# Reordering the SyncE queue of a hashed-attention and MLP kernel: row-turning reads and transfers ahead of stores and large loads

## The chip, the cores and the metric

The kernel runs on one core of one Trainium2 chip. The metric is device time in microseconds (us) of one execution, taken as the median of several runs.

## What is computed

There are 4 batches of 8 heads, 768 rows and head size 64. Queries and keys are hashed into buckets by the signs of six projections. A query attends only to keys of its own bucket; the attention output, with its heads side by side, is the x of a normalised two-layer MLP with a residual.

```
mask   = q_bucket[:, :, :, None] == k_bucket[:, :, None, :]
scores = np.where(mask, scale * q @ k.T, -1e9)
x      = softmax(scores) @ v                    # to (4, 768, 512)
xn     = (x - mean(x)) / sqrt(var(x) + 1e-6) * g_ln
out    = x + relu(xn @ w_ch1) @ w_ch2           # 512 -> 2048 -> 512
```

## The kernel before

**Units.** The 768 rows of each batch are cut into three units of 256 rows, so that there are 12 units u = 0 to 11. A unit goes through attention for two groups of four heads (g = 0, 1), then normalisation, then the MLP.

**Steps.** For each batch b and head group g, k and q rows are loaded in one transfer of 768 KB each (`LX.s.b.g.t`, line 508, with t = 0 for q and 1 for k) and transposed in 32x32 blocks on VectorE (`tu`, line 304). TensorE computes the projections (`hm`, line 526), VectorE makes sign bits of them (`bt`, line 307), and SyncE writes the bits to DRAM (`mw`, line 544) and reads them back in another arrangement with four small DMAs (`mr.s.b.g.i`, line 547, i = 0 to 3), into the tile G. These are the row-turning reads. The scores (`S`, line 570) start each accumulation with four matmuls that read all four parts of G, then ScalarE takes the exponential (`E`, line 576), and the values are multiplied in (`A`, line 595).

For each unit, VectorE normalises rows into xc (`ce.v.u.t`, line 630; t = 0, 1 are the two halves of 128 rows; a small GpSimd step `rs`, lines 635 and 636, comes ahead of it). From unit 2 on a DMA transpose turns each half into xnT (`fl.s.u.t`, line 639); these are the row-turning transfers. The first MLP layer (`F.t.u.p`, line 659, eight pieces p of a unit) reads both halves of xnT; its result is taken through relu by ScalarE or VectorE (`R`, lines 667 and 669). The second layer is a seven-product scheme on sums of blocks (`P`, line 725; sums `ss`, line 710; VectorE adds the products to x with `Y`, line 730). Last, four stores write the unit (`O.s.u.c`, line 744; 128 KB each; the last unit's at line 742). Values come with `lv.s.b.h.c` (line 467, 192 KB each).

**Order.** Nothing is reordered by a scheduler. A string ORDER lists all work word by word: name, engine, arguments. The engine letters are v VectorE, a ScalarE, p GpSimd, s SyncE, t TensorE. Each engine executes its words in the order of the string, and an instruction that waits holds back all behind it on the same engine. All words with an s are DMA issues on the one queue of SyncE (SPq in the profile). Another fixed string gives the buffer of each tile: TensorE's F, P and other small accumulators share two PSUM buffers, S and A share three.

```
with tc.manual_schedule():
    for word in ORDER.split():
        name, eng, *args = word.split(".")
        OPS[name](ENGINES[eng], *map(int, args))
```

Of the kernel before, what the change touches and what calls it, by code (L numbers as in the profile page):

```python
# [46 lines left out]
S.t.19.2 F.t.1.6 E.a.18.0 rs.p.2 F.t.1.3 CA.p.1.1.1 E.a.19.0 S.t.21.2 O.s.0.0 lv.s.1.4.1  # L47
E.a.19.1 A.t.19.2 E.a.21.0 R.v.1.6 sw.v.3.0 sw.v.2.0 E.a.21.1 F.t.1.0 R.a.1.0 lv.s.2.0.3
R.v.1.3 ce.v.2.1 sw.v.4.0 lv.s.1.4.0 ce.v.2.0 F.t.1.5 A.t.20.2 S.t.22.2 fl.s.2.1 tu.v.2.0.0.2
F.t.1.4 R.a.1.5 cv.p.1.4.0 A.t.18.2 LX.s.2.0.1 E.a.22.0 R.v.1.4 F.t.1.2 sp.t.1.0 sc.v.1.0  # L50
na.v.3.0 E.a.22.1 S.t.23.2 F.t.1.7 R.a.1.2 R.v.1.7 E.a.23.1 cv.v.1.4.2 E.a.23.0 F.t.1.1
sw.v.1.0 fl.s.2.0 R.a.1.1 nb.v.3.0 S.t.24.2 E.a.24.0 E.a.24.1 on.p.2 P.t.1.2 Y.v.1.2
F.t.2.1 R.a.2.1 su.p.1.4 S.t.26.2 lv.s.2.4.0 O.s.0.1 O.s.0.3 A.t.23.2 ss.v.1.1 P.t.1.1
P.t.1.5 ss.v.1.3 ss.v.1.2 tu.v.2.0.1.2 E.a.26.1 E.a.26.0 Y.v.1.1 lv.s.2.0.1 P.t.1.6 A.t.22.2
S.t.25.2 tu.v.2.0.0.3 ss.v.1.4 lv.s.2.4.3 E.a.25.0 Y.v.1.5 tu.v.2.0.0.0 Y.v.1.6 P.t.1.3 Y.v.1.3
# [13 lines left out]
F.t.3.7 R.a.3.7 F.t.3.0 tu.v.2.1.1.0 E.a.33.0 S.t.37.2 E.a.37.1 tu.v.2.1.1.1 E.a.37.0 tu.v.2.1.0.0  # L69
tu.v.2.1.1.3 tu.v.2.1.1.2 hm.t.2.1 O.s.2.0 CA.v.2.1.0 LX.s.3.0.0 bt.v.2.1 mw.s.2.1 mr.s.2.1.1 mr.s.2.1.3  # L70
S.t.38.2 F.t.3.5 R.v.3.0 A.t.34.2 R.a.3.5 F.t.3.3 CA.v.2.1.1 R.a.3.3 tu.v.3.0.1.0 E.a.38.1
A.t.35.2 F.t.3.4 A.t.33.2 O.s.2.2 nb.v.5.0 F.t.3.1 mr.s.2.1.2 R.a.3.4 na.v.5.1 tu.v.3.0.0.3
F.t.3.2 lv.s.3.4.1 E.a.38.0 R.a.3.1 rs.p.4 ce.v.4.1 S.t.36.2 P.t.3.2 R.a.3.2 E.a.36.1
nb.v.5.1 su.p.2.4 ss.v.3.1 Y.v.3.2 P.t.3.1 E.a.36.0 mr.s.2.1.0 S.t.39.2 E.a.39.1 E.a.39.0
O.s.2.3 ce.v.4.0 Y.v.3.1 nc.v.5.0 A.t.37.2 P.t.3.5 ss.v.3.2 ss.v.3.4 fl.s.4.1 LX.s.3.1.0
A.t.36.2 Y.v.3.5 cv.v.2.4.0 P.t.3.6 Y.v.3.6 P.t.3.3 A.t.38.2 ss.v.3.3 S.t.40.2 Y.v.3.3
E.a.40.0 E.a.40.1 P.t.3.7 nc.v.5.1 Y.v.3.7 tu.v.3.0.0.1 fl.s.4.0 F.t.4.3 ag.v.5.0 R.v.4.3
P.t.3.4 Y.v.3.4 O.s.3.1 O.s.3.0 S.t.41.2 E.a.41.1 E.a.41.0 sp.t.2.0 sc.v.2.0 F.t.4.0
ag.v.5.1 rs.p.5 F.t.4.4 R.a.4.4 na.v.6.0 R.v.4.0 O.s.3.3 ce.v.5.1 fl.s.5.1 S.t.44.2
E.a.44.1 tu.v.3.0.1.3 F.t.4.5 A.t.41.2 F.t.4.6 A.t.40.2 tu.v.3.0.0.2 E.a.44.0 R.a.4.6 tu.v.3.0.1.2  # L80
# [42 lines left out]
O.s.8.3 F.t.9.6 R.a.9.6 nb.v.11.0 ss.v.9.1 ss.v.9.2 S.t.70.2 E.a.70.1 A.t.71.2 ss.v.9.3  # L123
O.s.8.2 A.t.69.2 P.t.9.2 Y.v.9.2 ss.v.9.4 P.t.9.1 fl.s.10.0 E.a.70.0 Y.v.9.1 A.t.70.2
na.v.11.1 nb.v.11.1 fl.s.10.1 F.t.10.7 P.t.9.6 R.a.10.7 Y.v.9.6 nc.v.11.0 P.t.9.5 P.t.9.7
Y.v.9.5 Y.v.9.7 nc.v.11.1 P.t.9.3 Y.v.9.3 P.t.9.4 Y.v.9.4 O.s.9.3 O.s.9.0 O.s.9.2
F.t.10.6 R.a.10.6 ag.v.11.1 F.t.10.1 O.s.9.1 ag.v.11.0 rs.p.11 ce.v.11.0 fl.s.11.0 F.t.10.0
R.a.10.1 R.a.10.0 F.t.10.5 R.a.10.5 F.t.10.4 F.t.10.3 R.a.10.4 R.a.10.3 ce.v.11.1 fl.s.11.1
F.t.10.2 R.a.10.2 P.t.10.2 Y.v.10.2 F.t.11.4 R.a.11.4 ss.v.10.1 ss.v.10.2 P.t.10.1 Y.v.10.1
ss.v.10.4 P.t.10.5 Y.v.10.5 P.t.10.6 P.t.10.3 ss.v.10.3 Y.v.10.6 P.t.10.7 Y.v.10.3 F.t.11.0  # L130
R.a.11.0 Y.v.10.7 P.t.10.4 Y.v.10.4 O.s.10.2 F.t.11.2 R.a.11.2 F.t.11.5 R.a.11.5 F.t.11.7
# [10 lines left out]
    E="012302132023132032103230103231032031230120302123031230120321013202120320",  # L142
# [10 lines left out]
    rs="012102102102",  # L153
# [635 lines left out]
```

## Time and profile before

| | us |
|---|---|
| median of 3 runs | 294.99 |
| lowest and highest of them | 294.71, 295.28 |
| profiled execution, own time | 294.86 |
| its span, first to last instruction | 293.2 |
| mean granted TensorE clock | 1.000 |

The span is what the views of the profile divide up; the profiled execution's own time is 1.66 us longer than its span. In the profile PE is TensorE's matmuls, PEld its weight loads, DVE VectorE, ACT ScalarE, POOL GpSimd, SPq SyncE's DMA issues. A timeline row gives start, duration, engine, line, operation, output and inputs, the count of merged instructions, and in brackets the idle time before it with what ended it. Matmuls are pipelined, so that one row's duration reaches over the start of the next; the distance from start to start is what a group costs.

### The profile page before, as it was taken

The numbers are of one execution on the slowest core, as the hardware profiler recorded it, in microseconds if no ns is written. First come the engines' busy times: TensorE is split into PE (matmuls) and PEld (weight loads), VectorE is DVE, ScalarE is ACT, GpSimd is POOL, SyncE is SP. The second block draws the span as 40 slices with busy tenths as digits, with TensorE's granted clock in tenths as the row PEclk, the third lists the DMA queues.
The fourth block names the chain that finished last, engine by engine and source line by source line (L and its number), as shares of the span: only waits on it lengthen the run. The fifth ranks groups of instructions, "written<-read, shape, count | busy, mean of one in ns | idle before, by whom it ended". The sixth has DMA issues, their size and how long they took to land.

```text
span 293.2 us, 10524 instructions
## 1 busy us (share of the span) xinstructions
PE 285.6 (97%) x4650; PEld 227.7 (78%) x4650; DVE 206.8 (71%) x474; ACT 206.2 (70%) x236; POOL 54.0 (18%) x88
## 2 busy tenths in 40 slices
PE   8999999999999999999999999999999999999994
PEld 4677778648788887878778778877888878897883
DVE  4757899996769795797667995866666654773433
ACT  4689999998966978784865896887793694515240
POOL 5261325222423005000300107210010010000000
PEclk9999999999999999999999999999999999999999
DMA  6999997747744692362330352230410402304022
GB/s 223 302 319 250 216 277 133 139 134 171 174 122 131 134 307 76 127 189 51 98 82 1 83 132 63 60 61 3 92 37 2 74 2 52 78 6 104 2 72 73
DMA packets 31055, 34.10 MB, mean 116 GB/s; under 512 B 15521, under 2 KB 27809, under 8 KB 31010
## 3 DMA queue, kind: packets, MB, share of 16 engines
q1 hardware_dynamic: 25938, 28.72, 35.6%
q0 software_dynamic: 4224, 4.19, 8.9%
q8 instruction: 36, 0.59, 0.9%
q10 hardware_dynamic: 848, 0.53, 0.7%
q14 instruction: 9, 0.07, 0.1%
HBM read 27.86 MB, written 6.88 MB: 118 GB/s over the span
## 4 chain that ended last, share of the span: by engine, by line
PE 91%; DMA 3%; DVE 2%; SPq 1%; ACT 1%; issue 0%; ACTq 0%; DVEq 0%
PE f L659 27%; PE sc L570 18%; PE X L725 13%; PE acc L595 12%; PE Yb L725 7%; PE hp L526 3%; PE Ya L725 3%; PE hf L394 3%; PE f L674 2%; PE warm L363 1%; ACT E L576 1%; DMA G<-Bd 1%; DMA Bd<-B 1%; PE warm L366 1%; DMA xnT<-xc 1%; SPq L547 1%
## 5 line engine op out<-in xcount | busy, mean ns | idle before, releaser
L576 ACT ACTIVATE E<-sc,bias_sb 128x1024 bf16<-128x1024 f32 x144 | 153.1, 1111 | 36.0 <-PE sc L570 32.6
L659 PE MATMUL f<-xnT,w_sb 128*128 128x256 bf16 x768 | 94.2, 273 | 0.7 <-DMA xnT<-xc 0.6
L659 PEld LDWEIGHTS <-w_sb 128*128 128x128 bf16 x768 | 71.4, 98 | 13.6 <-issue 5.7
L667 ACT ACTIVATE hb<-f 128x512 bf16<-128x512 f32 x67 | 39.6, 598 | 34.5 <-PE f L659 34.5
L570 PE MATMUL sc<-qb,kb 32*128 32x256 bf16 x1152 | 52.5, 267 | 0.0
L595 PEld LDWEIGHTS <-E 128*128 128x128 bf16 x1152 | 40.8, 98 | 4.0 <-issue 2.5
L595 PE MATMUL acc<-vaug,E 128*128 128x65 bf16 x1152 | 43.7, 194 | 0.1
L570 PE MATMUL sc<-G 6*128 6x256 bf16 (+1 forms) x576 | 42.7, 273 | 1.1 <-ACT E L576 0.8
L725 PEld LDWEIGHTS <-hb 128*128 128x128 bf16 x352 | 33.4, 98 | 5.4 <-issue 1.3
L570 PEld LDWEIGHTS <-kb 32*128 32x128 bf16 x1152 | 30.5, 93 | 1.5
L635 POOL TENSOR_SCALAR rs<-mv 128x2 f32<-128x2 f32 x12 | 3.3, 277 | 150.4 <-DVE mv L624 150.4
L730 DVE TENSOR_TENSOR x<-X,x 128x256 f32<-128x256 f32 x44 | 18.4, 419 | 16.5 <-PE X L725 16.3
L570 PEld LDWEIGHTS <-G 6*128 6x128 bf16 (+1 forms) x576 | 16.0, 91 | 16.7 <-issue 13.3
L725 PEld LDWEIGHTS <-S 128*128 128x128 bf16 x264 | 25.0, 98 | 4.8 <-issue 1.4
L669 DVE TENSOR_SCALAR hb<-f 128x512 bf16<-128x512 f32 x29 | 19.7, 681 | 12.0 <-PE f L659 11.8
L304 DVE STREAM_TRANSPOSE T<-X 128x384 f32<-128x384 f32 (+2 forms) x52 | 26.1, 535 | 0.0
L725 PE MATMUL Yb<-w_sb,S 128*128 128x256 bf16 x176 | 22.9, 273 | 0.0
L608 DVE SCALAR_TENSOR_TENSOR y<-vsB,acc 128x520 f32<-128x520 f32 x24 | 16.5, 689 | 8.1 <-PE acc L595 7.8
L725 PE MATMUL X<-wt,hb 128*128 128x256 bf16 x168 | 21.8, 273 | 0.0
L617 DVE TENSOR_TENSOR x<-y,rc 128x512 f32<-128x512 f32 x24 | 17.8, 742 | 0.8
L621 DVE BATCH_NORM_STATS2 st<-x 128x6 f32<-128x256 f32 x48 | 17.4, 412 | 0.2
L730 DVE TENSOR_TENSOR x<-Yb,x 128x256 f32<-128x256 f32 x22 | 9.2, 420 | 9.5 <-PE Yb L725 9.5
(95 smaller groups left out, 268.3 us busy)
## 6 DMA issues: line engine op xcount, KB each, us to landing
out_dram<-x SPq DMA_DIRECT2D x45, 128.0 KB
X<-in_k_dram SPq DMA_DIRECT2D x7, 768.0 KB
vn<-in_v_dram SPq DMA_DIRECT2D x24, 192.0 KB
X<-in_q_dram SPq DMA_DIRECT2D x6, 768.0 KB
w_sb<-in_moe_w_ch_dram POOLq DMA_DIRECT2D x8, 512.0 KB, 10.8
vn<-in_v_dram SPq DMA_DIRECT2D x2, 768.0 KB
X<-in_q_dram SPq DMA_DIRECT2D x2, 512.0 KB
Bd<-B SPq DMA_DIRECT2D x6, 96.0 KB
```

The lines of the kernel that those rows point to most:

```text
L304: nc.vector.transpose(d[:, j], s[:, j, kj0 : kj0 + n])
L570: nc.tensor.matmul(sc(s, i // 2)[:, i % 2, 256 * kk : 256 * kk + 256], lh, rh, start=(rep == 0), stop=(rep == 2), skip_group_check=True,)
L576: nc.scalar.activation(E(s)[:, heads(h)], sc(s, h), AF.Exp, scale=EXP_SCALE, bias=bias_sb)
L595: nc.tensor.matmul(acc[:, qt, (D + 1) * i : (D + 1) * (i + 1)], E(s)[:, i, 256 * kk + P * qt : 256 * kk + P * qt + P], vaug(u // 3)[:, 4 * ...
L608: nc.vector.scalar_tensor_tensor(yt(u, g), vs, EPS_ROW, made[f"acc{u}{g}"][:, :, :A], op0=AOP.mult, op1=AOP.add,)
L617: nc.vector.tensor_tensor(xo, a[:, :, :, 0:D], rc.to_broadcast([P, 2, 4, D]), op=AOP.mult)
L621: nc.vector.bn_stats(stats(u)[:, qt, g], xt(u)[:, qt, 256 * g : 256 * g + 256])
L659: nc.tensor.matmul(f1[:, n].rearrange("p (t x) -> p t x", t=2), w1_sb[:, dt, P * nt : P * nt + P], xnT(u)[:, :, dt], start=(dt == 0), stop ...
L667: nc.scalar.activation(hb(u)[:, 2 * p : 2 * p + 2], f1, AF.Relu)
L669: eng.tensor_scalar_max(hb(u)[:, 2 * p : 2 * p + 2], f1, 0.0)
L725: nc.tensor.matmul(f2, lh[:, n], rh[:, n], start=(first and n == 0), stop=(n == 7), skip_group_check=True)
L730: nc.vector.tensor_tensor(x, made[f"{prod(u, k)}{u}"], x, op=AOP.add)
```

## The change

In four places of ORDER words with an s stand elsewhere. No word is added or taken out, and on TensorE, VectorE, ScalarE and GpSimd the order of the instructions is the same as before.

1. `LX.s.2.0.1` (768 KB of keys) goes from between `fl.s.2.1` and `fl.s.2.0` to behind `fl.s.2.0`.
2. `mr.s.2.1.2` and `mr.s.2.1.0` go ahead of `O.s.2.2` and `lv.s.3.4.1`: the four row-turning reads of batch 2, group 1, then stand together.
3. `LX.s.3.1.0` (768 KB of queries) goes from between `fl.s.4.1` and `fl.s.4.0` to behind `fl.s.4.0`.
4. The four stores `O.s.9.*` go from ahead of `fl.s.11.0` and `fl.s.11.1` to behind both.

```
-F.t.1.4 R.a.1.5 cv.p.1.4.0 A.t.18.2 LX.s.2.0.1 E.a.22.0 R.v.1.4 F.t.1.2 sp.t.1.0 sc.v.1.0
-na.v.3.0 E.a.22.1 S.t.23.2 F.t.1.7 R.a.1.2 R.v.1.7 E.a.23.1 cv.v.1.4.2 E.a.23.0 F.t.1.1
-sw.v.1.0 fl.s.2.0 R.a.1.1 nb.v.3.0 S.t.24.2 E.a.24.0 E.a.24.1 on.p.2 P.t.1.2 Y.v.1.2
+F.t.1.4 R.a.1.5 cv.p.1.4.0 A.t.18.2 E.a.22.0 R.v.1.4 F.t.1.2 sp.t.1.0 sc.v.1.0 na.v.3.0
+E.a.22.1 S.t.23.2 F.t.1.7 R.a.1.2 R.v.1.7 E.a.23.1 cv.v.1.4.2 E.a.23.0 F.t.1.1 sw.v.1.0
+fl.s.2.0 LX.s.2.0.1 R.a.1.1 nb.v.3.0 S.t.24.2 E.a.24.0 E.a.24.1 on.p.2 P.t.1.2 Y.v.1.2
...
-A.t.35.2 F.t.3.4 A.t.33.2 O.s.2.2 nb.v.5.0 F.t.3.1 mr.s.2.1.2 R.a.3.4 na.v.5.1 tu.v.3.0.0.3
-F.t.3.2 lv.s.3.4.1 E.a.38.0 R.a.3.1 rs.p.4 ce.v.4.1 S.t.36.2 P.t.3.2 R.a.3.2 E.a.36.1
-nb.v.5.1 su.p.2.4 ss.v.3.1 Y.v.3.2 P.t.3.1 E.a.36.0 mr.s.2.1.0 S.t.39.2 E.a.39.1 E.a.39.0
-O.s.2.3 ce.v.4.0 Y.v.3.1 nc.v.5.0 A.t.37.2 P.t.3.5 ss.v.3.2 ss.v.3.4 fl.s.4.1 LX.s.3.1.0
-A.t.36.2 Y.v.3.5 cv.v.2.4.0 P.t.3.6 Y.v.3.6 P.t.3.3 A.t.38.2 ss.v.3.3 S.t.40.2 Y.v.3.3
-E.a.40.0 E.a.40.1 P.t.3.7 nc.v.5.1 Y.v.3.7 tu.v.3.0.0.1 fl.s.4.0 F.t.4.3 ag.v.5.0 R.v.4.3
+A.t.35.2 F.t.3.4 A.t.33.2 mr.s.2.1.2 mr.s.2.1.0 O.s.2.2 nb.v.5.0 F.t.3.1 R.a.3.4 na.v.5.1
+tu.v.3.0.0.3 F.t.3.2 lv.s.3.4.1 E.a.38.0 R.a.3.1 rs.p.4 ce.v.4.1 S.t.36.2 P.t.3.2 R.a.3.2
+E.a.36.1 nb.v.5.1 su.p.2.4 ss.v.3.1 Y.v.3.2 P.t.3.1 E.a.36.0 S.t.39.2 E.a.39.1 E.a.39.0
+O.s.2.3 ce.v.4.0 Y.v.3.1 nc.v.5.0 A.t.37.2 P.t.3.5 ss.v.3.2 ss.v.3.4 fl.s.4.1 A.t.36.2
+Y.v.3.5 cv.v.2.4.0 P.t.3.6 Y.v.3.6 P.t.3.3 A.t.38.2 ss.v.3.3 S.t.40.2 Y.v.3.3 E.a.40.0
+E.a.40.1 P.t.3.7 nc.v.5.1 Y.v.3.7 tu.v.3.0.0.1 fl.s.4.0 LX.s.3.1.0 F.t.4.3 ag.v.5.0 R.v.4.3
...
-Y.v.9.5 Y.v.9.7 nc.v.11.1 P.t.9.3 Y.v.9.3 P.t.9.4 Y.v.9.4 O.s.9.3 O.s.9.0 O.s.9.2
-F.t.10.6 R.a.10.6 ag.v.11.1 F.t.10.1 O.s.9.1 ag.v.11.0 rs.p.11 ce.v.11.0 fl.s.11.0 F.t.10.0
-R.a.10.1 R.a.10.0 F.t.10.5 R.a.10.5 F.t.10.4 F.t.10.3 R.a.10.4 R.a.10.3 ce.v.11.1 fl.s.11.1
+Y.v.9.5 Y.v.9.7 nc.v.11.1 P.t.9.3 Y.v.9.3 P.t.9.4 Y.v.9.4 F.t.10.6 R.a.10.6 ag.v.11.1
+F.t.10.1 ag.v.11.0 rs.p.11 ce.v.11.0 fl.s.11.0 F.t.10.0 R.a.10.1 R.a.10.0 F.t.10.5 R.a.10.5
+F.t.10.4 F.t.10.3 R.a.10.4 R.a.10.3 ce.v.11.1 fl.s.11.1 O.s.9.3 O.s.9.0 O.s.9.2 O.s.9.1
```

The compiled program also makes each DMA of the hardware queues wait for the eighth DMA before it, since eight completion counters take turns. Moving a DMA moves these waits with it.

## Prediction

> **What bounds the kernel now.** I read the page first, then the waits of TensorE, then the timelines around each of them. From the page:
>
> ```profile
> span 293.2 us, 10524 instructions
> ...
> PE 285.6 (97%) x4650; PEld 227.7 (78%) x4650; DVE 206.8 (71%) x474; ACT 206.2 (70%) x236; POOL 54.0 (18%) x88
> ...
> PE 91%; DMA 3%; DVE 2%; SPq 1%; ACT 1%; issue 0%; ACTq 0%; DVEq 0%
> ```
>
> TensorE is busy in 285.6 of 293.2 us, and 91% of the chain that ended last runs through it. The other engines have 30% or more to spare. The change touches only SyncE, so it can pay only where TensorE itself stood still for one of SyncE's DMAs. The chain has 3% for DMA, so such places exist. The waits of PE from 60 us to the end (engine and line, what it waited for, us in total, times, longest):
>
> ```profile
> PE f L659 <- DMA xnT<-xc: 0.6, 1, 0.6
> PE sc L570 <- DMA G<-Bd: 0.3, 1, 0.3
> ```
>
> These two are all that PE itself shows in this stretch: once for a transposed half of xnT, once for a row-turning read into G. PEld shows a third, below. The idle time in brackets understates a stall, since matmuls overlap: the tail of one group hides the first part of a gap. So I measure each stall by the distance between the starts of two groups, against the same pair of groups where nothing waits.
>
> **Place 1: the load of keys behind the second transpose.** SyncE's timeline, then DVE's making of the second half of xc:
>
> ```profile
> 69.86 1.20 SPq L639 DMA_TRANSPOSE xnT<-xc  x1
> 71.11 0.58 SPq L508 DMA_DIRECT2D X<-in_k_dram  x1
> 71.79 1.20 SPq L639 DMA_TRANSPOSE xnT<-xc  x1
> ```
> ```profile
> 70.31 0.54 DVE L630 TENSOR_SCALAR xc<-x,mv,rs 128x512 bf16<-128x512 f32 x1
> ```
>
> The xc that `fl.s.2.0` reads is done at 70.85, so the transpose can be issued at 71.11 in the load's place, 0.68 us earlier. What waits for it, in the timelines of PE, of PEld, and of DVE for the load's reader:
>
> ```profile
> 77.72 1.05 PE L725 MATMUL Ya<-w_sb,hb 128*128 128x256 bf16 x8
> 78.75 1.05 PE L659 MATMUL f<-xnT,w_sb 128*128 128x256 bf16 x8
> ```
> ```profile
> 78.74 0.77 PEld L659 LDWEIGHTS <-w_sb 128*128 128x128 bf16 x8 [0.26 <-DMA xnT<-xc]
> ```
> ```profile
> 81.07 0.57 DVE L304 STREAM_TRANSPOSE T<-X 128x384 f32<-128x384 f32 x1
> ```
>
> F.2.1 starts 1.03 us after the product ahead of it. Undisturbed, eight matmuls of this shape take 0.87 or 0.88 us to the next group (126.48 to 127.36, quoted below, is 0.88). I take 0.87, and the stall is **0.16 us**. The transpose landed at 78.74 at the latest, 6.95 us after its issue. With 6.95 us again it would land at 78.06, ahead of the 78.59 at which TensorE would be ready; with the 2.48 us of another transpose (below) at 73.6. So the whole 0.16 goes. Bounds: 0 to 0.26, the bracket.
>
> The load's cost is what is added. Its issue moves to about 71.11 + 1.20 + 0.05 = 72.36, which is 1.25 us later. How long it travels, by the DMA column (last two: DMA share, GB/s):
>
> ```profile
> 76.00:77.00 1.00, 1.00 (x14) 0.72 (x15) 0.82 (x2) 1.00 (x2) 0.70 (x1) 1.00 0.04 4
> ```
>
> From 76.00 almost nothing moved, so the load issued at 71.11 had its bytes across within 4.9 us, hence by 77.3 in the new order. Its first reader is the DVE transpose at 81.07, `tu.v.2.0.1.2`, which comes to 80.9 once TensorE runs 0.16 us earlier: 3.6 us of cover. Even if the load took the 6.95 us of the transpose it lands at 79.3, with 1.6 us left. One more wait moves with the load: the value load `lv.s.2.0.0` is the eighth DMA behind it now and waits for its landing; that load's buffer is not read before the other quarters of the tile have come. I cost the moved load at nothing.
>
> The Trainium skill, page "DMA: Bandwidth & Descriptors", section "Queues, rings and completion order", says that each DMA engine consumes the descriptors of a ring in order. The trace agrees in so far as the transpose behind the load took 6.95 us and another one, with no load just ahead, 2.48. By that rule the load now pays for the transpose put ahead of it; the sum stays as it is, since 1.6 us or more of cover is left, but this is what makes the slower rival below possible.
>
> **Place 2: the four reads of G together.** PE's timeline at the stall, the same pair of groups where nothing waits, and SyncE's timeline:
>
> ```profile
> 126.48 1.05 PE L725 MATMUL Ya<-w_sb,hb 128*128 128x256 bf16 x8
> 127.36 1.04 PE L725 MATMUL X<-w_sb,hb 128*128 128x256 bf16 x8
> 128.70 0.29 PE L570 MATMUL sc<-G 6*128 6x256 bf16 x4 [0.30 <-DMA G<-Bd]
> ```
> ```profile
> 112.31 1.04 PE L725 MATMUL X<-wt,hb 128*128 128x256 bf16 x8
> 113.28 0.29 PE L570 MATMUL sc<-G 6*128 6x256 bf16 x4
> ```
> ```profile
> 123.82 0.43 SPq L744 DMA_DIRECT2D out_dram<-x  x1
> 124.30 0.67 SPq L547 DMA_DIRECT2D G<-Bd  x1
> 125.08 0.37 SPq L467 DMA_DIRECT2D vn<-in_v_dram  x1
> 125.50 0.67 SPq L547 DMA_DIRECT2D G<-Bd  x1
> 126.22 0.44 SPq L744 DMA_DIRECT2D out_dram<-x  x1
> 126.70 1.27 SPq L639 DMA_TRANSPOSE xnT<-xc  x1
> 128.01 0.57 SPq L508 DMA_DIRECT2D X<-in_q_dram  x1
> ```
>
> The undisturbed distance is 113.28 - 112.31 = 0.97, here it is 1.34: a stall of **0.37 us**. The chain of waits puts it on the last of the four reads:
>
> ```profile
> 125.50 3.16 DMA G<-Bd
> ```
>
> In the new order the third read is issued at 123.82 and the fourth at 123.82 + 0.67 + 0.05 = 124.54, which is 0.96 earlier. With the same 3.16 us it lands at 127.70, and TensorE is ready at 128.33; it should be shorter, since the value load and one store are no longer between. So all 0.37 goes. Lower bound 0.30 by the bracket; above 0.37 there is nothing. The next limit is a PSUM buffer that ACT's exponential of S.36 gives back for A.37, which comes behind S.39:
>
> ```profile
> 126.60 2.12 ACT L576 ACTIVATE E<-sc,bias_sb 128x1024 bf16<-128x1024 f32 x2 [0.19 <-PE sc L570]
> ```
>
> It ends at 128.72, after S.39 starts but before its end, so it hinders nothing at 128.33. The store and the value load move back by two issues (about 1.4 and 0.7 us) and their sum with the next store fills the same time, so the transpose at 126.70 stays. The value load's readers need the other quarters of that tile too, of which the next, `lv.s.3.4.3`, is issued here:
>
> ```profile
> 165.01 0.43 SPq L467 DMA_DIRECT2D vn<-in_v_dram  x1
> ```
>
> So its 0.7 us cost nothing.
>
> **Place 3: the load of queries behind the transpose.** The load is issued at 128.01 now. The transpose takes its place, as soon as its xc is done (about 128.5), and the load follows at about 129.7, 1.7 us later. TensorE shows no wait for this transpose, so nothing is gained. The load's first reader, in DVE's timeline:
>
> ```profile
> 148.18 0.83 DVE L304 STREAM_TRANSPOSE T<-X 128x128 f32<-128x128 f32 x2
> ```
>
> At 129.7 + 6.95 = 136.7 it has landed by a long estimate from place 1: 11 us of cover. Cost **0**.
>
> **Place 4: four stores behind the last two transposes.** SyncE, the chain, DVE's making of xc (both halves), PE, and ACT's last relu of unit 10:
>
> ```profile
> 262.91 3.07 SPq L744 DMA_DIRECT2D out_dram<-x  x4
> 266.09 2.51 SPq L639 DMA_TRANSPOSE xnT<-xc  x2
> 277.67 1.73 SPq L744 DMA_DIRECT2D out_dram<-x  x4
> ```
> ```profile
> 267.39 2.48 DMA xnT<-xc
> ```
> ```profile
> 264.20 1.00 DVE L630 TENSOR_SCALAR xc<-x,mv,rs 128x512 bf16<-128x512 f32 x2 [1.13 <-POOL rs L636]
> ```
> ```profile
> 268.37 1.04 PE L725 MATMUL Ya<-w_sb,hb 128*128 128x256 bf16 x8
> 270.01 1.03 PE L659 MATMUL f<-xnT,w_sb 128*128 128x256 bf16 x8 [0.60 <-DMA xnT<-xc]
> ```
> ```profile
> 268.57 0.60 ACT L667 ACTIVATE hb<-f 128x512 bf16<-128x512 f32 x1 [0.28 <-PE f L659]
> ```
>
> F.11.4 starts 1.64 us after the product; undisturbed it is 0.87: a stall of **0.77 us**. The first xc half is done near 264.7 and the second at 265.2, while SyncE is still issuing stores until 265.98. In the new order the first transpose goes out at about 264.75, the second 1.3 us later at 266.05, where it is 267.39 now; with the same 2.48 us it lands at 268.53, ahead of 269.24. What is late next is F.11.4's PSUM buffer, which the relu at 268.57 gives back at 269.17: just in time. So 0.77 goes; bounds 0.60 by the bracket and 0.77. The stores go out from about 267.3 and need 3.1 us. No buffer is reused behind them (unit 9's x is never overwritten), the next stores come at 277.67, and the end lies at 293.2: cost 0.
>
> **Sum.** 0.16 + 0.37 + 0.77 = 1.30 us, and 0 for what is moved back. TensorE is the chain between the places, and the work of DVE, ACT and SyncE at the later places follows it, so that each gain moves all that comes after. The profiled execution took 294.86: 294.86 - 1.30 = 293.56, and its span 293.2 - 1.3 = 291.9. The median of the runs is 0.13 higher, so I forecast 294.99 - 1.30 = 293.69, rounded **293.7 us** (0.44% less). 0.2%, or 0.6 us, is about what a measurement of this kernel can tell from no change.
>
> **Rivals.**
>
> *Only the last stall pays.* The first two gains (0.53 us) lie 140 us and more ahead of the end; ACT or DVE may hold TensorE at some later wait, and then only place 4 counts: 294.99 - 0.77 = 294.2, or 294.4 with 0.60. For it: ACT is busy 70% on average, and at place 2 its exponential ends only shortly ahead of A.37. Against it: PE waits for no other engine after 60 us in the list above.
>
> *The waits come back.* F.11.4 has the PSUM buffer of the relu as its next limit and the xc halves behind GpSimd's step; if the second transpose again lands near 270 because the first one's issue is held, all that is left is places 1 and 2: 294.99 - 0.53 = 294.5, no difference that can be told. Against it: xc is ready 1.3 us before the issue now.
>
> *The load of keys becomes the bound: slower.* The transpose of place 1 took 6.95 us although little moved from 76.00 on, and the trace does not tell what held it. If that hold now falls on the load, with two transposes ahead of it in the queue, it lands late and DVE stands at 81.07, with `Y` and the sums for TensorE's products behind it. It decides from a landing at 80.9, that is 8.5 us after the issue. Each further us costs TensorE up to one: 11.8 us of travel cost 3.3, less the 1.14 of places 2 and 4, so 294.99 + 2.2 = 297.2; 10.3 us cost 1.8, giving 295.7. Against it: 6.95 us is the longest seen here.
>
> *The change does not do what it says.* The order of SyncE's issues shows the four moves and the other engines unchanged, so I give it 1 in 100, at 295.0.
>
> **How the numbers follow.** The forecast has 0.66, with its own range 293.2 to 294.1 (the bounds of the three terms, 0.90 to 1.40, and 0.4 more below for the spread of the runs). Only the last stall: 0.17, of which 0.11 lies under 294.4 and counts as faster, 0.06 within 0.2%. The waits come back: 0.07, within. No move: 0.01, within. The late load: 0.09, of which 0.08 slower and 0.01 within. Faster is 0.66 + 0.11 = 0.77; same 0.06 + 0.07 + 0.01 + 0.01 = 0.15; slower 0.08. The range reaches over the forecast and most of the second case: 293.2 to 294.5, leaving out some 2 in 10.
>
> **What would show it.** In the profile after, PE's waits for xnT and G after 60 us are gone; F.2.1 follows its product by 0.87, S.39 by 0.97, F.11.4 by 0.87; the chain has no DMA between 119 and 129 and none at 267; TensorE's last product ends 1.3 us earlier. Wrong would be: a DVE wait for X near 81 or 148, a wait of the same length at F.11.4 with another releaser, or TensorE gaining at the three places and losing the time at ACT later.

## The result, and the profile after

| | before | after |
|---|---|---|
| median of 15 runs, us | 294.99 | 293.46 |
| lowest to highest, us | 293.51 to 297.25 | 292.44 to 295.73 |
| profiled execution, own time, us | 294.86 | 293.50 |
| its span, us | 293.2 | 291.8 |

The ratio after to before is 0.9944, 95% interval 0.9921 to 0.9967: 1.65 us less, between 0.97 and 2.33 (the two medians lie 1.53 us apart). From the page after, the span, the busy times, and the chain that ended last by engine:

```profile
span 291.8 us, 10523 instructions
...
PE 285.1 (98%) x4648; PEld 228.0 (78%) x4650; DVE 205.9 (71%) x474; ACT 206.1 (71%) x236; POOL 53.8 (18%) x88
...
PE 95%; DVE 2%; ACT 1%; issue 0%; ACTq 0%; DVEq 0%
```

DMA has left the chain altogether, and PE is 95% of it where it was 91%. PE's waits over the whole span of the kernel after:

```profile
PE warm L363 <- DVE bias_sb L320: 1.1, 1, 1.1
PE sc L570 <- ACT E L576: 0.8, 3, 0.4
PE ft L644 <- DVE xc L628: 0.2, 1, 0.2
```

Neither xnT nor G is among them. PE's timeline after, around the three places (answers for three windows):

```profile
77.65 1.05 PE L725 MATMUL Ya<-w_sb,hb 128*128 128x256 bf16 x8
78.53 1.04 PE L659 MATMUL f<-xnT,w_sb 128*128 128x256 bf16 x8
...
127.14 1.04 PE L725 MATMUL X<-w_sb,hb 128*128 128x256 bf16 x8
128.11 0.29 PE L570 MATMUL sc<-G 6*128 6x256 bf16 x4
...
267.78 1.04 PE L725 MATMUL Ya<-w_sb,hb 128*128 128x256 bf16 x8
268.65 1.04 PE L659 MATMUL f<-xnT,w_sb 128*128 128x256 bf16 x8
...
286.48 1.04 PE L725 MATMUL Yc<-wt,hb 128*128 128x256 bf16 x8
```

The three distances from start to start are 0.88, 0.97 and 0.87 us, where they were 1.03, 1.34 and 1.64. Against before, F.11.4 comes 1.36 us earlier (268.65 for 270.01). The last product, which stood at 287.83 before, comes 1.35 us earlier, so nothing was given back in the 18 us between. SyncE after:

```profile
69.80 2.52 SPq L639 DMA_TRANSPOSE xnT<-xc  x2
72.37 0.57 SPq L508 DMA_DIRECT2D X<-in_k_dram  x1
...
119.50 0.34 SPq L544 DMA_DIRECT2D Bd<-B  x1
122.66 2.80 SPq L547 DMA_DIRECT2D G<-Bd  x4
...
264.22 2.50 SPq L639 DMA_TRANSPOSE xnT<-xc  x2
```

Both pairs of transposes go out back to back. The key load is at 72.37 (forecast 72.36), and the transposes of unit 11 start at 264.22 instead of 266.09. The key load's first reader on DVE, without a wait in brackets:

```profile
81.00 0.57 DVE L304 STREAM_TRANSPOSE T<-X 128x384 f32<-128x384 f32 x1
```

The traces also keep the increments of the DMAs' completion counters, which none of the views above prints. The last increment of a DMA is its landing; where a landing below stands in no line, it was read from these counters. By them the key load landed 4.48 us after its issue, at 76.85, and so 4.15 us ahead of this reader.

### The profile page after: what moved, and what is told of

The parts are those of the page before. It is cut to its first block, busy times and chain, and to the rows that moved or that the text cites. A ratio compares the mean times of both kernels' runs of the same rounds, so it can differ in the third digit from the quotient of the medians.

```text
span 291.8 us, 10523 instructions
## 1 busy us (share of the span) xinstructions
PE 285.1 (98%) x4648; PEld 228.0 (78%) x4650; DVE 205.9 (71%) x474; ACT 206.1 (71%) x236; POOL 53.8 (18%) x88
## 4 chain that ended last, share of the span: by engine, by line
PE 95%; DVE 2%; ACT 1%; issue 0%; ACTq 0%; DVEq 0%
PE f L659 30%; PE sc L570 18%; PE X L725 13%; PE acc L595 12%; PE Yb L725 7%; PE Ya L725 3%; PE hp L526 3%; PE hf L394 3%; PE f L674 2%; PE warm L363 1%; ACT E L576 1%; PE warm L366 1%; DVE xnT L652 0%; PE hf L405 0%; PE vp L487 0%; PE Yc L725 0%
## 5 line engine op out<-in xcount | busy, mean ns | idle before, releaser
L617 DVE TENSOR_TENSOR x<-y,rc 128x512 f32<-128x512 f32 x24 | 16.6, 692 | 0.8
L480 POOL TENSOR_TENSOR t<-vn 128x768 f32<-128x768 f32 x6 | 11.4, 1896 | 25.0 <-DMA vn<-in_v_dram 25.0
```

Of the source, the lines that this page charges most:

```text
L617: nc.vector.tensor_tensor(xo, a[:, :, :, 0:D], rc.to_broadcast([P, 2, 4, D]), op=AOP.mult)
```

## The experiments

A stall below is the distance from start to start less that of an undisturbed pair (0.87, 0.97 and 0.87 us), as in the prediction. In some of these kernels ORDER is wrapped in fewer lines, so that a code line has a number 7 lower. Where a kernel has one run, the table sets it beside 295.08, the median of 23 runs of the kernel before measured with it.

**Each place alone**, on the kernel before. The edit of the first:

```
-fl.s.2.1 ... LX.s.2.0.1 ... fl.s.2.0 R.a.1.1
+fl.s.2.1 ... fl.s.2.0 LX.s.2.0.1 R.a.1.1
```

> Only place 1: the key load LX.s.2.0.1 behind fl.s.2.0, all else as before. Each stall is read as the distance from start to start of two neighbouring groups of TensorE. My theory (each place removes its own stall, and the gains add): the distance from the product Ya to F.2.1 falls from 1.03 to 0.87 us, the stalls at S.39 (1.34) and F.11.4 (1.64) stay within 0.1 us, and the span is 0.1 to 0.2 us shorter than before's 293.2, with the scatter of single executions on top. The rival that early gains are given back: 0.87 at F.2.1, but a stall at S.39 or F.11.4 that is longer by as much. The rival that the key load becomes the bound: DVE shows a wait for X at 81 us.

The second, third and fourth:

```
-O.s.2.2 nb.v.5.0 F.t.3.1 mr.s.2.1.2 ... lv.s.3.4.1 ... mr.s.2.1.0
+mr.s.2.1.2 mr.s.2.1.0 O.s.2.2 nb.v.5.0 F.t.3.1 ... lv.s.3.4.1 ...
```
```
-fl.s.4.1 LX.s.3.1.0 ... fl.s.4.0
+fl.s.4.1 ... fl.s.4.0 LX.s.3.1.0
```
```
-O.s.9.3 O.s.9.0 O.s.9.2 ... O.s.9.1 ... fl.s.11.0 ... fl.s.11.1
+... fl.s.11.0 ... fl.s.11.1 O.s.9.3 O.s.9.0 O.s.9.2 O.s.9.1
```

> Only place 2: the four row-turning reads of batch 2, group 1, stand together. My theory: the distance from the product to S.39 falls from 1.34 to 0.97 us, F.2.1 keeps its 1.03 and F.11.4 its 1.64 within 0.1 us, the time falls by 0.37 us (ratio 0.9987, too small for the interval). If early gains are given back: the time stays, and F.11.4 or a later group waits 0.37 us longer.

> Only place 3: the query load LX.s.3.1.0 behind fl.s.4.0. My theory: nothing changes, all three stalls stay (1.03, 1.34, 1.64 us within 0.1) and DVE shows no wait for X near 148 us. The rival that moving a load is never free: DVE waits for X at 148 us, or the span is over 0.5 us longer.

> Only place 4: the four stores of unit 9 behind both transposes of unit 11. My theory: the distance from the product Ya to F.11.4 falls from 1.64 to 0.87 us, the stalls at F.2.1 and S.39 stay within 0.1 us, the time falls by 0.77 us (ratio 0.9974). The rival that only the last stall pays: the ratio is that of the whole change, 0.9944. The rival that the wait comes back with another releaser: F.11.4 still 1.2 us or more behind its product, ratio near 1.

| kernel | stall at F.2.1 | at S.39 | at F.11.4 | time |
|---|---|---|---|---|
| before | 0.16 | 0.37 | 0.77 | 1 |
| place 1 alone | 0.02 | 0.79 | 0.39 | one run, 295.1 us beside 295.08 |
| place 2 alone | 0.43 | 0 | 0 | 0.9977 (0.9952 to 1.0001) |
| place 3 alone | 0.02 | 1.18 | 0.66 | one run, 295.34 us beside 295.08 |
| place 4 alone | 0.01 | 0.93 | 0 | 0.9983 (0.996 to 1.0006) |
| after | 0.01 | 0 | 0 | 0.9944 (0.9921 to 0.9967) |

The edits at places 2 and 4 leave no stall at their own place, as expected. The load of place 3 was free: DVE's list of waits in that run has no wait for X near 148. But my expectation that the other stalls would stay within 0.1 us failed in every row. Place 2 alone shows nothing at F.11.4, where its order is still the old one, and S.39 stalled for 0.79 to 1.18 us in three kernels that leave it as it was. PE's timeline in the kernel with place 3 alone:

```profile
127.19 1.04 PE L718 MATMUL X<-w_sb,hb 128*128 128x256 bf16 x8
129.34 0.29 PE L563 MATMUL sc<-G 6*128 6x256 bf16 x4 [1.11 <-DMA G<-Bd]
```

and in the kernel with place 2 alone, at the stores' place that it leaves untouched:

```profile
268.74 1.04 PE L718 MATMUL Ya<-w_sb,hb 128*128 128x256 bf16 x8
269.61 0.60 PE L652 MATMUL f<-xnT,w_sb 128*128 128x256 bf16 x4
```

Both have the same code at that place as before, with 2.15 us instead of 1.34, and 0.87 instead of 1.64. Either one change moves a stall elsewhere, or a stall is drawn anew in each execution.

**The kernel before, twice more**, unchanged.

> The kernel before once more, unchanged, for a second profile. In the four runs that change one place, the stalls at the unchanged places were not those of before's profile: 0.01 to 0.43 us at F.2.1 (before 0.16), 0.79 to 1.18 at S.39 (before 0.37), 0 to 0.66 at F.11.4 (before 0.77). My theory now: each execution draws its stalls anew, from how long SyncE's stores take to issue and how long the bits take to land in DRAM; the kernel before would show 0 to 0.5, 0.3 to 1.3 and 0 to 0.8 us, not the same three numbers again. The rival: before's three numbers are fixed (within 0.1 us: 0.16, 0.37, 0.77) and the single-place kernels differ because of their change.

> A third profile of the kernel before, for the same question: drawn anew (three stalls that again differ by 0.2 us or more from the other two profiles, S.39 by 0.3 to 1.3 us) or fixed at 0.16, 0.37 and 0.77 us within 0.1.

The stalls were 0.01, 1.26 and 0.38 us in the second profile, and 0.01, 1.43 and 0.05 in the third. The rival falls: with no change of the code the numbers are not 0.16, 0.37 and 0.77 again. The two new profiles are alike at the first two places and differ by 0.33 us at the third, so I had asked for more scatter between them than there was, and 1.43 lies beyond the 1.3 that I gave for S.39. What is drawn at place 2 shows in SyncE's timeline of the first profile of before, quoted in the prediction from 123.82 on, which begins

```profile
117.00 0.36 SPq L508 DMA_DIRECT2D X<-in_q_dram  x1
119.71 0.34 SPq L544 DMA_DIRECT2D Bd<-B  x1
122.38 1.39 SPq L547 DMA_DIRECT2D G<-Bd  x2
```

and in the third:

```profile
116.07 0.36 SPq L508 DMA_DIRECT2D X<-in_q_dram  x1
118.78 0.34 SPq L544 DMA_DIRECT2D Bd<-B  x1
122.53 1.39 SPq L547 DMA_DIRECT2D G<-Bd  x2
```

From the write of the bits to the first read it took 2.67 us in one and 3.75 in the other, 1.08 more; the stall at S.39 is 1.06 longer (1.43 against 0.37). So the time until the write lands goes straight into the stall. It is not a time of the small write by itself. The first line of both views is a load of 768 KB (`LX.s.3.0.0`), issued 2.71 us ahead of the write, and in all twelve profiles of this document the write lands 0.30 to 0.33 us behind that load. The six profiles with the old order at place 2, in us:

| kernel | load LX.s.3.0.0, issue to landing | stall at S.39 |
|---|---|---|
| before | 5.03 | 0.37 |
| place 1 alone | 5.34 | 0.79 |
| place 4 alone | 5.60 | 0.93 |
| place 3 alone | 6.06 | 1.18 |
| before, second | 6.08 | 1.26 |
| before, third | 6.09 | 1.43 |

The stall rises with the time of this load in all six. No run moves the load, so it is not shown that moving it would end the stall, and what makes it take 5.03 us in one execution and 6.09 in another stays open.

At place 4 it is the issue of one DMA that is drawn. In the second and then in the third profile of before:

```profile
263.16 1.72 SPq L744 DMA_DIRECT2D out_dram<-x  x4
265.06 3.40 SPq L639 DMA_TRANSPOSE xnT<-xc  x2
```

```profile
263.04 1.72 SPq L744 DMA_DIRECT2D out_dram<-x  x4
264.95 3.06 SPq L639 DMA_TRANSPOSE xnT<-xc  x2
```

In both the four stores take 1.72 us and leave SyncE free when xc is ready, but then the first transpose takes long to issue: 2.09 and 1.76 us instead of 1.20, and F.11.4 stalls 0.38 and 0.05. In the first profile it was the fourth store (1.77 us of the 3.07), and the stall was 0.77. In each of the six profiles with the old order at place 4 one of these five issues takes 1.39 to 2.09 us. What holds it is not shown by an experiment. The traces show a coincidence: in all six, one packet of 16 KB on the instruction queue, 0.90 to 1.59 us long, starts at 264.04 to 264.90 while the stores are under way; two or three stores get the last of their 16 counts 1.0 to 1.9 us behind the others; and the held issue ends 0.2 to 1.1 us behind the packet. In the kernel after, the packet runs from 263.44 to 264.66 with no store under way, and no issue is held. No run moves the packet.

**A load ahead of both transposes of unit 11**, in the kernel after:

```
-fl.s.11.0
+LX.s.3.1.1 fl.s.11.0
```

> The changed kernel with one more 768 KB load on SyncE's queue right ahead of the two transposes of unit 11 (it reads keys of batch 3 again into a buffer that nobody reads any more). It tells whether a transfer ahead in the queue costs the transposes its issue or its bytes. If only the issue counts (0.4 to 0.6 us, and SyncE is free from 250 us on, so that even this is hidden): F.11.4 stays 0.87 us behind its product, time as the changed kernel. If the transposes stand behind the load's bytes (a load of this size needed up to 4.9 us from issue to quiet): the load, issued as soon as the transposes of unit 10 are out, at about 252 us, is over before the xc halves are ready at 263.6, so it must again be without effect. Both say no effect here unless SyncE's issue itself is held; an F.11.4 later than 1.0 us behind its product would show that.

Stalls 0.01, 0 and 0; ratio to before 0.9948 (0.9919 to 0.9977). The load was out at 251.93, 11.5 us before the transposes. The run tells nothing about order in the queue, as its expectation had to admit; it stands as a second timing of the change's three places.

**The key load later still**, in the kernel after:

```
-fl.s.2.0 LX.s.2.0.1 ... O.s.0.1 O.s.0.3
+fl.s.2.0 ... O.s.0.1 O.s.0.3 LX.s.2.0.1
```

> The changed kernel with the key load LX.s.2.0.1 moved on, behind the stores O.s.0.1 and O.s.0.3: its issue goes from 72.37 to about 78.7 us. It prices the rival in which this load becomes the bound. By the 4.9 us from issue to quiet that a load of this size needed, it lands near 84 us, while its reader on DVE stands at 81.0. My theory: DVE waits 2 to 4 us for X, and TensorE loses nearly that, less some 0.5 us of room at the products behind it: 1.5 to 3.5 us longer than the changed kernel, that is near or above before (ratio 0.999 to 1.006). If the cover was longer than I read it: no wait of DVE, time as the changed kernel (0.9944).

The ratio to before is 1.0103 (1.0058 to 1.0147), beyond my upper end of 1.006, which the interval just reaches. From the answers of SyncE, DVE and PE:

```profile
79.38 0.45 SPq L501 DMA_DIRECT2D X<-in_k_dram  x1
```
```profile
85.89 0.58 DVE L297 STREAM_TRANSPOSE T<-X 128x384 f32<-128x384 f32 x1 [4.18 <-DMA X<-in_k_dram]
```
```profile
82.22 1.04 PE L718 MATMUL Yb<-w_sb,S 128*128 128x256 bf16 x8
86.83 1.87 PE L718 MATMUL X<-wt,S 128*128 128x256 bf16 x8 [3.57 <-DVE x L723]
88.49 1.09 PE L588 MATMUL acc<-vaug,E 128*128 128x65 bf16 x16
```

The mechanism of the slower rival is real. The load landed 6.41 us after its issue, and DVE stood 4.18 us for it. The 4.9 us that I had read from the DMA column were too short: by the completion counters the same load had needed 6.39 us in the first profile of before. TensorE lost 86.83 - 82.22 - 0.87 = 3.74 us, which is DVE's wait less 0.4 us of room. But it lost more behind that: the eight matmuls at 86.83 took 1.66 us to the next group instead of 0.87. The windows say why (the number before the last two is the granted clock):

```profile
84.00:86.00 2.00, 0.00 (x0) 0.00 (x0) 0.11 (x1) 0.00 (x0) 0.00 (x0) 1.00 1.04 261
86.00:87.00 1.00, 0.17 (x2) 0.11 (x2) 1.00 (x3) 0.00 (x0) 0.00 (x0) 0.75 0.82 222
87.00:88.00 1.00, 1.00 (x6) 0.76 (x5) 1.00 (x3) 0.00 (x0) 0.00 (x0) 0.50 0.32 118
88.00:89.00 1.00, 1.00 (x13) 0.82 (x12) 0.91 (x3) 0.00 (x0) 0.45 (x1) 0.50 0.00 0
89.00:90.00 1.00, 1.00 (x23) 0.79 (x24) 0.16 (x1) 0.00 (x0) 1.00 (x1) 0.54 0.00 0
```

After 3.57 us of idleness the granted clock was 0.50 for about 3.4 us, from about 86.5 on. That does not happen in every execution: of the nine runs behind the ratio, three have a mean granted clock of 1.000 and took 295.65 to 295.91 us, which is inside what I expected (1.5 to 3.5 us above the changed kernel's 293.46); the six with 0.991 to 0.994 took 296.79 to 299.81.

**A load between two transposes, and a load ahead of the last read**, both in the kernel after:

```
-fl.s.11.1
+LX.s.3.1.1 fl.s.11.1
```

> The changed kernel with one more load of 768 KB between the two transposes of unit 11 (keys of batch 3 again, into a buffer that nobody reads any more), as place 1 had a load between its two. Issue alone: the second transpose goes out 0.65 us later, near 266, and lands 2.5 us after: F.11.4, ready at 268.6, stalls 0 to 0.2 us. Bytes ahead in the queue: the load is quiet up to 4.9 us after its issue at about 265.2, so the transpose lands at 270.5 to 272.7 and F.11.4 stalls 2 to 4 us, with more lost behind if the granted clock falls as it did after the stall of 3.7 us in the late-keys run.

```
-mr.s.2.1.2 mr.s.2.1.0 ... fl.s.4.0 LX.s.3.1.0
+mr.s.2.1.2 LX.s.3.1.0 mr.s.2.1.0 ... fl.s.4.0
```

> The changed kernel with the query load LX.s.3.1.0 (768 KB) moved ahead of the last of the four row-turning reads of place 2. Issue alone: that read goes out 0.6 us later, near 125.4, and lands at most 3.2 us after: S.39, ready at 128.1, stalls 0 to 0.5 us. Bytes ahead in the queue: the read lands behind the load, 129.5 to 131.5, and S.39 stalls 1.5 to 3.5 us, that is 2.5 to 4.5 us from start to start of the two groups.

PE and the chain with the load between the transposes:

```profile
267.22 1.04 PE L718 MATMUL Ya<-w_sb,hb 128*128 128x256 bf16 x8
270.51 1.03 PE L652 MATMUL f<-xnT,w_sb 128*128 128x256 bf16 x8 [2.26 <-DMA xnT<-xc]
```
```profile
265.57 4.81 DMA xnT<-xc
```

and with the load ahead of the read:

```profile
127.91 1.04 PE L718 MATMUL X<-w_sb,hb 128*128 128x256 bf16 x8
131.85 0.29 PE L563 MATMUL sc<-G 6*128 6x256 bf16 x4 [2.90 <-DMA G<-Bd]
```
```profile
126.74 5.07 DMA G<-Bd
```

The stalls are 3.29 - 0.87 = 2.42 us and 3.94 - 0.97 = 2.97 us, inside what the bytes would give (2 to 4, 1.5 to 3.5) and far outside what the issue alone would (0.2, 0.5). The transpose needs 4.81 us to land and a read of 24 KB 5.07, where the counters of the kernel after have 2.44 and 2.23; each lands 0.5 to 0.6 us behind the load. So in these two runs, of one profile each, a small transfer pays for the bytes of a load issued ahead of it, not only for its issue. This is what the Trainium skill says on the page "DMA: Bandwidth & Descriptors", section "Queues, rings and completion order": each DMA engine takes the descriptors of a ring in order. These two runs agree with it. They do not tell the order in the queue from a mere sharing of the DMA engines, since no run puts the load on another queue.

## Why the prediction was right

- **Place 1.** Right in direction and small. F.2.1's stall was 0.16 us in the profile that I read; in the six executions with the old order it was 0.16, 0.01, 0.01, 0.43, 0.02 and 0.01, a mean of 0.11. As four of the six are 0.01 or 0.02, the 0.02 with place 1 alone and the 0.01 after do not show by themselves that the edit did it. The key load cost nothing, as forecast: its reader on DVE did not wait. The forecast had its bytes across within 4.9 us of the issue, where the counters put its landing in that profile at 6.39; behind both transposes it needed 4.48, so the cover was long enough all the same.
- **Place 2.** The mechanism held: the last of the four reads was late behind a store and a value load, and standing together they are in time in every run with the new order that has no load between. The six profiles with the old order have 2.90 to 3.16 us from issue to landing of the last read, right behind the value load; with the four reads together it is 2.22 to 2.26 in five profiles, as for most of the other reads. The 0.96 us of earlier issue, with which the forecast was worked out, would not have covered stalls of 1.18 to 1.43; the earlier landing, which it only mentions, was needed too. The size failed: 0.37 us was one draw, the smallest of six (0.37, 1.26, 1.43, 0.79, 1.18, 0.93), whose mean is 0.99.
- **Place 3.** 0, as forecast.
- **Place 4.** The mechanism held in the profile that was read: SyncE was still issuing stores when xc was ready. In three of the six profiles the stores were out in time, and the first transpose's own issue was held. With the new order no issue was held, and F.11.4 stalls 0 in all three profiles where it was read (after, place 4 alone, the load ahead of both transposes). Again the size was a draw, the largest of six (0.77, 0.38, 0.05, 0.39, 0, 0.66; mean 0.38).
- **The sum.** 293.7 us was forecast, with a range of 293.2 to 294.5, and 293.46 was measured. The gain of 1.30 us came from one profile, 1.48 is the sum of the three means, and 1.65 (0.97 to 2.33) was measured. That the forecast was so near is in part luck: two terms were off, one too small by 0.6 us and one too large by 0.4, and nearly made up for each other. That the gains add is in keeping with the single places: 0.0023 and 0.0017 with about 0.0004 for place 1's 0.11 us make 0.0044 of 0.0056, but each of those intervals reaches past no change, and they do not prove it. What is shown is that after has none of the three stalls and that its last product starts 1.35 us earlier, of which 0.07 were there ahead of place 1 (77.65 for 77.72).
- **"Only the last stall pays"** fell: in the profile after, S.39 starts 0.59 us earlier than before (128.11 for 128.70), and 140 us on the product ahead of F.11.4 is still 0.59 us earlier (267.78 for 268.37). By the mean stalls place 2 is the largest term; the times of places 2 and 4 alone do not tell the two apart. **"The waits come back"** fell with PE's list of waits after. **The late key load** did not occur in the change, since the load came 7 us earlier than in the run that provoked it. There its price was above one us for each us of delay in the runs in which the clock fell, and as I wrote in the others.

## What to carry to other kernels

On a queue that carries both, put the small transfers that an engine is about to wait for ahead of the large loads and stores that have several us of cover; what they save is the bytes ahead of them, not only the issue. Read a stall that ends with a DMA in several profiles before it is given a price: the code was the same, and one place drew 0.37 to 1.43 us. Then look for what stands ahead of the DMA that is late: here the write of the bits goes out behind a load of 768 KB, which is the next order to try and which no run has tried. And check the cover of what is moved back, since a load that comes too late costs its delay and, where the clock falls, more.

## What the runs showed of the hardware that was not expected

- **The clock after a stall.** An idle TensorE of 3.57 us (late key load) and of 2.90 us (load ahead of the read) was followed by a granted clock of 0.50 for about 3.4 us; after 2.26 us of idleness (load between the transposes) the clock stayed at 1.00. The run with 2.90 us of idleness:

```profile
132.00:133.00 1.00, 1.00 (x37) 0.76 (x29) 0.00 (x0) 0.20 (x1) 0.00 (x0) 1.00 0.90 156
133.00:134.00 1.00, 1.00 (x15) 0.77 (x12) 0.00 (x0) 1.00 (x2) 0.00 (x0) 0.59 0.08 16
134.00:135.00 1.00, 1.00 (x10) 0.75 (x9) 0.00 (x0) 0.92 (x1) 0.00 (x0) 0.50 0.00 0
135.00:136.00 1.00, 1.00 (x18) 0.94 (x16) 0.90 (x2) 0.00 (x0) 0.00 (x0) 0.50 0.00 0
136.00:137.00 1.00, 1.00 (x9) 0.76 (x8) 0.00 (x0) 0.00 (x0) 0.00 (x0) 0.70 0.00 0
```

  The Trainium skill, page "TensorE: Matmul & The Clock Gate", section "Part 1: The HAM clock gate (the "warmup" mystery)", has the clock fall after an idle window of about 3.4 us; here 2.90 us was enough, and in that run the fall came more than 1 us after TensorE had started again. With 3.57 us it came about 0.3 us before the restart at 86.83.
- **A small DMA behind a load lands with the load.** The write of 96 KB of bits at place 2, issued 2.71 us behind a load of 768 KB, landed 0.30 to 0.33 us behind it in all twelve profiles, while the load itself took 4.43 to 6.20 us from issue to landing. In the three profiles of before, with no change of the code, it took 5.03, 6.08 and 6.09.
- **One DMA issue among five was held** at place 4 in all six profiles with the old order: four stores of 128 KB took 1.72 to 3.07 us to issue and the two transposes behind them 2.51 to 3.40, in the same place of the same code.
